# A copy from bank to bank in the first FFN layer: the second product accumulates onto the first's

## The chip, the core and the metric

The kernel runs on one core of a Trainium2 chip. The metric is the device time of one execution in microseconds (us), the median of the runs shown. Beside it stands one profiled execution with its trace: the page and the answers of the trace come from that one, and its times are counted from the start of its span.

## The reference

For x of 2048 tokens with 576 features the kernel computes `x + attention(LN(x)) @ wo + FFN(LN(x))`. The attention is local and dilated (32 heads of 18 features, 8 keys per token at a step of 2). The FFN is what the change touches:

```python
h = jnp.einsum("bsd,df->bsf", x, w1) + b1          # 576 -> 4608
sp = jnp.log1p(jnp.exp(-jnp.abs(h))) + jnp.where(h > 0, h, jnp.zeros_like(h))
act = h * jnp.tanh(sp)                               # Mish
return jnp.einsum("bsf,fd->bsd", act, w2)            # 4608 -> 576
```

## The kernel before

**Precision.** Every fp32 matrix is split into a high part and a low part, and a product is made of three matmuls per 128 rows of depth: high x high, high x low, low x high. ScalarE casts the high part (L254 for weights, L720 for activations, L807 for sums), VectorE or POOL subtracts it for the low part (L255, L721, L813).

**Halves, blocks, pairs.** The tokens are two halves (hf 0 and 1) of 1024, each of two blocks (b) of 512. The 4608 hidden features are 18 pairs (q) of two tiles (j) of 128. For one pair and one half the first layer is a 2x2 problem (block b, tile j), computed with seven products instead of eight, in the manner of Strassen and Winograd. The products are summed in three PSUM banks of 128 x 512 fp32, called cur[1], cur[2], cur[3] in the code (tag "h", four buffers) and `h` in the profile. Four more banks (tag "out") take the second layer's results `po`. A product (`prod`, L669) is six matmuls; some are followed by two more for the last 64 features (`rest`, L675).

**The parts of a pair** (`m1_part`, L727). Part 0 is the first product into bank 1, its copy to SBUF by `take` (ScalarE, L703, the tile is named c11, `c` or a raw tile in the profile), then the second product into bank 2, and `mish(hf, q, 0, 0, ...)`. Part 1 is the third product into bank 3. Part 2 accumulates onto bank 1, copied as c21; part 3 accumulates onto bank 1 again, copied as c22; part 4 accumulates onto bank 3 and part 5 onto bank 1. A pair has 50 matmuls of 512 columns.

**What `mish` does.** With a copy `t` given, VectorE adds the bank to it (L714), ScalarE applies Mish to the sum in SBUF (L715), casts it (L720), and POOL makes the low part (L721). Without one (`fresh`, block 0, tile 1), ScalarE reads the bank with Mish, and there is no add. In the second half, pairs 0 to 8, the activations are kept raw (tiles `ra`, `rm`, `rt`), and the second layer is itself a seven-product scheme: sums of raw activations (L801), high and low parts `u` (L807, L813), matmuls with prepared weights `pw` (L859, the items "N"), and adds to `accP` (L865).

**The order of the work.** A plan, a list of items, is written out in the order of TensorE's work. In the first half from pair 2 on it is: part 0, part 1, chunk, part 2, chunk, part 3, chunk, part 4, chunk, part 5, where a chunk is 24 matmuls of 288 columns of an earlier pair's second layer (L767) with its adds (L771). The last pairs of the second half have chunks too (L880, adds L883). Work of other engines hangs on the items: `bg` (loads, casts, attention steps, put there by `before`), `pend` (the rest of `mish`, run at the start of the next item, called `held` there), and `soon` (a softmax exponential with its activation table, L558, and transposes of attention, run at the start of the next item, called `first` there). Attention steps are hung on items `cuts`, worked out from the items' costs `PART` and `US`. Each engine runs its queue in the order of issue. Line 1544 ff. fixes that order within an item:

```python
for i, (fns, bg, _) in enumerate(plan):
    first, soon[:] = soon[:], []
    held, pend[:] = pend[:], []
    for fn in first + bg + (fns + held if i == at["m", 0, 1, 0] else held + fns):
        fn()
```

Of the kernel before, what the change touches and what calls it, by code (L numbers as in the profile page):

```python
# [18 lines left out]
NH = 2  # L19
# [7 lines left out]
NP = NF // 2  # L27
# [12 lines left out]
def block_kernel(ctx: ExitStack, tc: tile.TileContext, x, wq, wo, w1, b1, w2, mask, out):  # L40
    nc = tc.nc
# [624 lines left out]
    def prod(ph, wt, off, X, hi, lo, first, last):  # L666
        seq = [(off + k, wl, xs + k) for k in range(2) for wl, xs in ((0, hi), (0, lo), (1, hi))]
        for i, (wk, wl, xs) in enumerate(seq):
            nc.tensor.matmul(ph, wt[:, wl, wk * P:(wk + 1) * P], X[:, xs, :],  # L669
                             start=first and i == 0, stop=last and i == len(seq) - 1,  # L670
                             skip_group_check=True)

    def rest(ph, wt, off, X, xs):
        for wl in range(2):
            nc.tensor.matmul(ph, wt[:, wl, off * P:(off + 1) * P], X[:, xs, :], start=False, stop=wl == 1,  # L675
                             skip_group_check=True)
# [21 lines left out]
    def take(hf, q, name):  # L698
        if seven(hf, q):
            t = cur[name] = raw_act(q, *dict(c11=(0, 0), c21=(1, 0), c22=(1, 1))[name])  # L700
        else:
            t = cur[name] = sb.tile([P, TB], F32, tag="mn", bufs=5, name=f"{name}_{hf}_{q}")
        nc.scalar.copy(t, cur[1])  # L703

    def mish(hf, q, b, j, ph, t=None):
        f = 2 * (Q1[q] if hf else q) + j
        n = f"{hf}_{b}_{f}"
        fresh = t is None
        if fresh:
            t = raw_act(q, b, j) if seven(hf, q) else sb.tile([P, TB], F32, tag="mn", bufs=5, name=f"mn_{n}")  # L710

        def run():
            if not fresh:
                nc.vector.tensor_tensor(out=t, in0=ph, in1=t, op=ALU.add)  # L714
            nc.scalar.activation(t, ph if fresh else t, AF.Mish, bias=b1c[:, f:f + 1])  # L715
# [4 lines left out]
            nc.scalar.copy(a[:, 0, :], t)  # L720
            nc.gpsimd.tensor_tensor(out=a[:, 1, :], in0=t, in1=a[:, 0, :].bitcast(F32), op=ALU.subtract)  # L721
        if q or b != j:
            pend.append(run)
        else:
            late.append(run)

    def m1_part(hf, q, part):  # L727
        X0, X1 = XTs[hf, 0], XTs[hf, 1]
        if part == 5 and late:
            for fn in late[::-1]:  # L730
                fn()
            late.clear()
        wa, wc, t0, t1 = (done.get((k, hf, q)) for k in ("wa", "wc", "t0", "t1"))
        if part == 0:
            prod(bank(hf, q, 1), wa, 0, X0, 0, 5, True, True)
            take(hf, q, "c11")
            prod(bank(hf, q, 2), wa, 2, X0, 2, 7, True, False)
            rest(cur[2], wa, 4, X0, 4)
            mish(hf, q, 0, 0, cur[2], cur["c11"])
        elif part == 1:  # L740
            prod(bank(hf, q, 3), t1, 0, X1, 0, 5, True, True)
        elif part == 2:
            prod(cur[1], t0, 2, Ss[hf, 1], 0, 2, False, True)
            take(hf, q, "c21")
        elif part == 3:
            prod(cur[1], t0, 0, Ss[hf, 0], 0, 2, False, False)
            rest(cur[1], wc, 2, X1, 4)
            take(hf, q, "c22")
        elif part == 4:
            prod(cur[3], t1, 2, X1, 2, 7, False, False)  # L750
            rest(cur[3], wa, 4, X1, 4)
            mish(hf, q, 1, 0, cur[3], cur["c21"])
        else:
# [400 lines left out]
    def qi(hf, g, b, jj, alias=None):  # L1154
        add(("q", hf, g, b, jj), lambda: qkv_item(hf, g, b, jj), alias=alias)
# [4 lines left out]
    def mi(hf, q, part, alias=None):  # L1160
        add(("m", hf, q, part), lambda: m1_part(hf, q, part), alias=alias)
# [68 lines left out]
    def quad(hf, q):  # L1230
        if q == 0:
            for part, ids in ((0, (0,)), (2, (1, 2)), (1, (3, 4)), (3, (5, 6)), (5, (7, 8)), (4, (9,))):
                for p_ in {}.get(part, ()) if hf else ():
                    zi(JB - 1, p_)
                if part == 5 and hf == 0:
                    qi(hf, NQ - 1, 0, JB - 1)
                mi(hf, 0, part)
                for i in ids:
                    at["s", hf, 0, i] = len(plan) - 1
            return  # L1240
        if hf and q <= 2 * OC + 1:
            C9 = list(((1,0),(1,1),(0,0),(0,1)))
            if q == 1:
                seq = ((0, (0,)), (2, (1, 2)), (1, (3, 4)), (3, (5, 6)), (4, (7, 8)), (5, (9,)))
            elif q == 2 * OC:
                seq = ((0, (0,)), (1, (1,)), ("N", (2,)), (2, (3,)), ("N", (4,)), (3, (5,)), ("N", (6,)), (4, (7,)), ("N", (8,)),
                                (5, (9,)), ("N", ()))
            elif q == 2 * OC + 1:
                seq = (("N", (0,)), (0, ()), ("N", (1,)), (1, ()), (2, (2,)), ("C", (3,)), (3, (4,)), ("C", (5,)), (4, (6,)), ("C", (7,)), (5, (8,)), ("C", (9,)))
            elif q % 2 == 0:  # L1250
                seq = (0, 1, "N", 2, "N", 3, "N", 4, "N", 5) if q > 2 else (0, 2, "N", 1, "N", 3, "N", 4, "N", 5)
                seq = [(p_, (i,)) for i, p_ in enumerate(seq)]
            else:
                seq = [(p_, (i, 9)[0:1 + (i == 8)]) for i, p_ in enumerate((0, 1, 2, "N", 3, "N", 4, "N", 5))]
            for part, ids in seq:
                if part == "N":
                    pi()
                elif part == "C":
                    pr_(1, q - 1, *C9.pop(0))
                else:  # L1260
                    for p_ in {4:(3,)}.get(part, ()) if q == 1 else ():
                        zi(JB - 1, p_)
                    mi(1, q, part)
                for i in ids:
                    at["s", 1, q, i] = len(plan) - 1
            return
        k = 0
        late_chunks = q == 1 or (hf, q) == (1, NP - 1)
        for i, part in enumerate((0, 1, 2, None, 3, None, 4, None, 5, None) if late_chunks else
                                 (0, 1, None, 2, None, 3, None, 4, None, 5)):  # L1270
            if (hf, q) == (0, NP - 1) and i in (5, 7, 9):
                tr(0, (i - 5) // 2)
            alias = ("s", hf, q, i)
            if part is not None:
                mi(hf, q, part, alias)
            else:
                pr_(hf, q - 1, *CHUNKS[k], alias)
                k += 1
# [87 lines left out]
    for q in range(1, 2 * OC + 1):  # L1366
        i = spot(0, q, (3,2)[q > 1])
# [5 lines left out]
    i = spot(0, NP - 1, 0)  # L1373
# [5 lines left out]
    i = at["q", 1, 0, 1, 1]  # L1379
# [4 lines left out]
    i = spot(0, 9, 4)  # L1384
# [44 lines left out]
    i = at["q", 0, 1, 1, 0]  # L1429
# [3 lines left out]
    i = at["q", 0, 3, 1, 0]  # L1433
# [5 lines left out]
    i = at["q", 1, 0, 1, 1]  # L1439
# [9 lines left out]
    for n in range(0, JB, 2):  # L1449
        i = at["q", 0, 1, 0, n]  # L1450
# [4 lines left out]
    for n in range(TJ):  # L1455
        i = spot(0, 2 + n, 2)
# [3 lines left out]
    i = spot(0, NP - 2, 0)  # L1460
# [7 lines left out]
    for n, (name, pr) in enumerate((name, pr) for name in ("P4", "P5", "P2", "P3") for pr in range(2)):  # L1468
        i = items[dict(P4=0, P5=2, P3=2, P2=3)[name]][2] + pr
# [23 lines left out]
    cuts = [[], []]  # L1493
# [101 lines left out]
```

## Time and profile before

| | |
|---|---|
| three runs | 1117.51, 1117.38, 1114.83 us; median 1117.38 |
| the profiled execution | 1114.25 us |
| its span | 1112.5 us |
| granted TensorE clock, mean | 1.000 |
| matmuls of 512 columns in the first layer | 36 pairs of 50 |
| adds of VectorE at L714 on a copy `c` in SBUF | 81, 684 ns each |
| copies of a bank by ScalarE at L703 into `c` | 81, 586 ns each |

The page's first part has the engines' busy times, the fourth the chain of work that ended last. The view by stretches gives busy times of every engine between two times. The view of waits lists what an engine waited for, with total, count and the longest. The timeline lists instructions in order of start: start, duration of the row, engine, line, operation, and in brackets the idle time before it with what ended it. A row with x6 stands for six instructions in a row, and its duration reaches from the first one's start to the last one's end. PE is TensorE's matmul, PEld its weight load, DVE is VectorE, ACT is ScalarE, POOL is GpSimd. "Half 2, pair 6" is hf 1, q 6.

### The profile page before, as it was taken

To read this page: it belongs to the slowest core of one execution; us is meant where nothing else is said; L and a number is where in the kernel's file an instruction comes from. 1 tells how busy PE (TensorE), PEld (TensorE's weight loads), DVE (VectorE), ACT (ScalarE), POOL (GpSimd) and SP (SyncE) were. 2 spreads that over 40 slices of the span, in tenths; PEclk is the share of its full clock that TensorE was granted. 3 is DMA by queue.
4 is the path that set the end of the run, shared out by engine and by line. 5 is a ranking of instruction groups with operands and counts; after the bars stand their busy time and mean duration, and the time that the engine had idled before them with its cause. 6 is when DMAs were issued, how large, how long until landed. Compare 5 with 4: busy or idle time off the path is not lost.

```text
span 1112.5 us, 18203 instructions
## 1 busy us (share of the span) xinstructions
PE 1101.6 (99%) x6550; PEld 1015.2 (91%) x6550; DVE 849.5 (76%) x1367; ACT 499.5 (45%) x917; POOL 790.8 (71%) x639
## 2 busy tenths in 40 slices
PE   9999999999999999999999999999999999999998
PEld 8999899999999999999999889989989999999998
DVE  6369788888889888897656577786776677777786
ACT  5544655544454544555333354433433344343353
POOL 2479777766679688785788676666688976867532
PEclk9999999999999999999999999999999999999999
DMA  6899696868777758675597898565664657776574
GB/s 202 283 312 316 225 356 214 285 233 276 258 242 264 268 208 301 249 249 204 190 323 241 245 375 307 211 196 196 220 222 170 209 195 223 244 288 219 171 232 142
DMA packets 178270, 271.60 MB, mean 244 GB/s; under 512 B 53218, under 2 KB 120068, under 8 KB 178180
## 3 DMA queue, kind: packets, MB, share of 16 engines
q1 hardware_dynamic: 178180, 270.44, 71.6%
q8 instruction: 52, 0.85, 0.3%
q14 instruction: 38, 0.31, 0.1%
HBM read 160.39 MB, written 110.00 MB: 243 GB/s over the span
## 4 chain that ended last, share of the span: by engine, by line
PE 87%; POOL 6%; DVE 3%; issue 2%; ACT 1%; DMA 0%; SPq 0%; POOLq 0%; DVEq 0%; ACTq 0%
PE h L669 28%; PE po L767 21%; PE pq L348 9%; PE po L880 9%; PE po L859 6%; PE h L675 5%; PE o L1063 5%; PE z L446 3%; POOL pv L571 2%; POOL accP L868 1%; POOL pr L533 1%; POOL act L721 1%; POOL s L620 1%; DMA acc<-in_x 0%; PE ta L75 0%
## 5 line engine op out<-in xcount | busy, mean ns | idle before, releaser
L767 PEld LDWEIGHTS po<-w,act 128*128 128x128 f32 x1728 | 236.4, 188 | 6.0 <-POOL act L721 0.4
L767 PE MATMUL po<-w,act 128*128 128x288 f32 x1728 | 240.7, 295 | 0.1
L533 POOL TENSOR_TENSOR pr<-q,kv 128x576 f32<-128x576 f32 x128 | 196.9, 1563 | 8.5 <-DMA q<-q_d 5.0
L721 POOL TENSOR_TENSOR act<-c,act 128x512 fp32r<-128x512 f32 x81 | 107.3, 1325 | 128.6 <-ACT act L720 128.6
L571 POOL TENSOR_TENSOR pv<-L,kv 128x576 f32<-128x576 f32 x128 | 177.9, 1484 | 26.1 <-DVE L L564 21.2
L771 DVE TENSOR_TENSOR acc<-po,acc 128x288 f32<-128x288 f32 x288 | 119.4, 448 | 29.9 <-PE po L767 29.0
L348 PE MATMUL pq<-wq,xt 128*128 128x432 f32 x672 | 136.5, 361 | 1.0 <-ACT xt L81 1.0
L880 PEld LDWEIGHTS po<-w,act 128*128 128x128 f32 x960 | 130.9, 188 | 4.6 <-DVE accP L883 1.8
L880 PE MATMUL po<-w,act 128*128 128x288 f32 x960 | 133.5, 295 | 1.0 <-DVE accP L883 1.0
L348 PEld LDWEIGHTS pq<-wq,xt 128*128 128x128 f32 x672 | 125.0, 188 | 8.0 <-ACT xt L81 1.8
L715 ACT ACTIVATE c<-c,b1c 128x512 f32<-128x512 f32 x81 | 58.7, 725 | 140.7 <-DVE c L714 140.4
L669 PE MATMUL h<-xt,t 128*128 128x512 f32 x432 | 110.6, 391 | 0.5 <-DVE rt L714 0.3
L669 PE MATMUL h<-S,t 128*128 128x512 f32 x432 | 110.5, 391 | 0.0
L577 DVE TENSOR_REDUCE og<-pv 128x144 f32<-128x1152 f32 x64 | 86.0, 1345 | 25.7 <-POOL pv L571 25.6
L669 PE MATMUL h<-xt,wa 128*128 128x512 f32 x432 | 104.1, 390 | 0.0
L538 DVE TENSOR_REDUCE L<-pr 128x64 f32<-128x1152 f32 x64 | 85.8, 1341 | 23.8 <-POOL pr L533 23.7
L703 ACT COPY c<-h 128x512 f32<-128x512 f32 x81 | 47.4, 586 | 124.1 <-PE h L675 73.0
L859 PEld LDWEIGHTS po<-pw,u 128*128 128x128 f32 x672 | 92.2, 188 | 5.4 <-DVE u L813 2.1
L859 PE MATMUL po<-pw,u 128*128 128x288 f32 x672 | 94.3, 295 | 2.5 <-DVE u L813 1.6
L669 PEld LDWEIGHTS h<-xt,wa 128*128 128x128 f32 x432 | 80.9, 188 | 17.0
L669 PEld LDWEIGHTS h<-xt,t 128*128 128x128 f32 x432 | 79.0, 188 | 15.7 <-DVE rt L714 0.7
L883 DVE TENSOR_TENSOR accP<-po,accP 128x288 f32<-128x288 f32 x160 | 68.9, 452 | 29.8 <-PE po L880 28.2
(228 smaller groups left out, 1853.8 us busy)
## 6 DMA issues: line engine op xcount, KB each, us to landing
kv<-kv_d SPq DMA_DIRECT2D x64, 396.0 KB, 5.1
kept_t<-t SPq DMA_DIRECT2D x36, 512.0 KB, 4.8
t<-kept_t SPq DMA_DIRECT2D x36, 512.0 KB, 6.7
rw<-in_w SPq DMA_DIRECT2D x36, 320.0 KB, 4.4
kept_wa<-wa SPq DMA_DIRECT2D x18, 640.0 KB, 4.7
kept_w<-w SPq DMA_DIRECT2D x20, 576.0 KB, 4.1
wa<-kept_wa SPq DMA_DIRECT2D x18, 640.0 KB, 5.2
w<-kept_w SPq DMA_DIRECT2D x20, 576.0 KB, 4.1
```

Of the source, the lines that this page charges most:

```text
L348: nc.tensor.matmul(pq[:, 0:432], XT[:, xi, tok], wt[wi][:, hl, 0:432], start=i == 0, stop=i == len(seq) - 1)
L533: nc.gpsimd.tensor_tensor(out=pr[:, x:x + hh], in0=q[:, j0 + x:j0 + x + hh, None, :].to_broadcast([P, hh, W, CU]), in1=win(kt, 0, CU, j0 + ...
L538: nc.vector.tensor_reduce(L[:, k, j0:j0 + hj].rearrange("p j w h -> p (j w h)"), pr.rearrange("p j w (h d) -> p (j w h) d", h=2), axis=AX, ...
L571: nc.gpsimd.tensor_tensor(out=pr[:, x:x + hj].rearrange("p j d w -> p j w d"), in0=L[:, k, x:x + hj, :, h:h + 1].to_broadcast([P, hj, W, DH]),
L577: nc.vector.tensor_reduce(og[:, c0:c0 + DH, :].rearrange("p d j -> p j d"), pr, axis=AX, op=ALU.add)
L669: nc.tensor.matmul(ph, wt[:, wl, wk * P:(wk + 1) * P], X[:, xs, :], start=first and i == 0, stop=last and i == len(seq) - 1, skip_group_ch ...
L721: nc.gpsimd.tensor_tensor(out=a[:, 1, :], in0=t, in1=a[:, 0, :].bitcast(F32), op=ALU.subtract)
L767: nc.tensor.matmul(po, acts[hf, q, b, j][:, al, tok], done["w2", hf, 2 * q + j][:, wl, c * HC:(c + 1) * HC], start=i == 0, stop=i == 5)
L771: nc.vector.tensor_tensor(out=t, in0=po, in1=t, op=ALU.add)
L859: nc.tensor.matmul(po, units[e, k, qq][:, al, tok], w[:, qq, wl, :], start=i == 0, stop=i == 5)
L880: nc.tensor.matmul(po, acts[hf, q, b, j][:, al, tok], done["w2", hf, 2 * q + j][:, wl, c * HC:(c + 1) * HC], start=i == 0, stop=i == 5)
L883: nc.vector.tensor_tensor(out=t, in0=po, in1=t, op=ALU.add)
```

## The change

From pair 2 on, in both halves, `take` of c11 goes. ScalarE copies bank 1, which holds the first product, straight into bank 2, and the second product accumulates onto it there. `mish` for block 0, tile 0 is then fresh: ScalarE reads bank 2 with Mish, and the add goes. So that the second product needn't follow the first at once, the third product now stands between them: part 1 holds the third and then the second product. Banks are taken in the order 2, 3, 1 at the start of part 0.

```diff
-            prod(bank(hf, q, 1), wa, 0, X0, 0, 5, True, True)
-            take(hf, q, "c11")
-            prod(bank(hf, q, 2), wa, 2, X0, 2, 7, True, False)
-            rest(cur[2], wa, 4, X0, 4)
-            mish(hf, q, 0, 0, cur[2], cur["c11"])
+            for n in (2, 3, 1):
+                bank(hf, q, n)
+            prod(cur[1], wa, 0, X0, 0, 5, True, True)
+            if q > 1:
+                nc.scalar.copy(cur[2], cur[1])
+            else:
+                take(hf, q, "c11")
         elif part == 1:
-            prod(bank(hf, q, 3), t1, 0, X1, 0, 5, True, True)
+            half = (hf, q) == (1, 0)
+            prod(cur[3], t1, 0, X1, 0, 5, True, True, range(3) if half else range(6))
+        elif part == 6:
+            prod(cur[3], t1, 0, X1, 0, 5, True, True, range(3, 6))
...
+        if part == 7 or (part == 1 and q and (hf, q) != (1, 1)):
+            prod(cur[2], wa, 2, X0, 2, 7, q < 2, False)
+            rest(cur[2], wa, 4, X0, 4)
+            mish(hf, q, 0, 0, cur[2], None if q > 1 else cur["c11"])
...
-    PART = (3.2, 1.4, 1.4, 1.8, 1.8, 1.8)
+    PART = (1.4, 3.2, 1.4, 1.8, 1.8, 1.8, 0.7, 1.8)
...
+    seeded = {at["m", hf, q, 0] for hf in range(NH) for q in range(2, NP)}
     for i, (fns, bg, _) in enumerate(plan):
         first, soon[:] = soon[:], []
         held, pend[:] = pend[:], []
-        for fn in first + bg + (fns + held if i == at["m", 0, 1, 0] else held + fns):
+        if i in seeded and i not in cuts[0] + cuts[1]:
+            order = bg + held + fns + first
+        else:
+            order = first + bg + (fns + held if i == at["m", 0, 1, 0] else held + fns)
+        for fn in order:
             fn()
```

Pair 0 of both halves keeps its copy to SBUF and its add, with the second product as part 7 right behind part 0; half 2, pair 1 has it behind part 2. In half 2, pair 0, the third product is cut in two, and its second three matmuls (part 6) come between parts 3 and 5. A few items of half 2, pairs 1, 2 and 9, change places, and some attention steps move by an item. All lines behind L675 get numbers higher by 1 to 20; the copy into the bank is L740.

**TensorE and ScalarE, half 1, pair 4.** TensorE's queue at the end of pair 3 and through the first products of pair 4, before. 2226 is bank 1 of pair 4, 2235 bank 2, 2254 bank 3:

```order
L669 MATMUL h_0_3_1940<-S_0_796,wc_3_1747 128x512 x6
L675 MATMUL h_0_3_1940<-xt_1_511,wc_3_1747 128x512 x2
L669 MATMUL h_0_4_2226<-xt_0_227,wa_4_1961 128x512 x6
L669 MATMUL h_0_4_2235<-xt_0_227,wa_4_1961 128x512 x6
L675 MATMUL h_0_4_2235<-xt_0_227,wa_4_1961 128x512 x2
L669 MATMUL h_0_4_2254<-xt_1_511,t_0_4_2132 128x512 x6
```

The same place in the change (2225 is bank 1, 2223 bank 2, 2224 bank 3):

```order
L670 MATMUL h_0_3_1941<-S_0_796,wc_3_1746 128x512 x6
L676 MATMUL h_0_3_1941<-xt_1_511,wc_3_1746 128x512 x2
L670 MATMUL h_0_4_2225<-xt_0_227,wa_4_1952 128x512 x6
L670 MATMUL h_0_4_2224<-xt_1_511,t_0_4_2130 128x512 x6
L670 MATMUL h_0_4_2223<-xt_0_227,wa_4_1952 128x512 x6
L676 MATMUL h_0_4_2223<-xt_0_227,wa_4_1952 128x512 x2
```

The third product's six matmuls moved ahead of the second product's eight. ScalarE's queue around the copy of the first product, before (`L_1` is a softmax tile, `w`, `wa` and `t` are weights of later pairs, `mn_0_7` is tile 1 of pair 3, `c_0_4` is c11 of pair 4):

```order
L558 ACT_TABLE_LOAD
L558 ACTIVATE L_1_1599<-L_1_1599 128x256
L254 CAST w_0_8_2214<-rw_8_2071 128x576
L715 ACT_TABLE_LOAD
L715 ACTIVATE mn_0_7_2212<-h_0_3_1940,b1c 128x512
L720 CAST act_0_7_2223<-mn_0_7_2212 128x512
L703 COPY c_0_4_2233<-h_0_4_2226 128x512
L254 CAST wa_5_2247<-rw_10_2136 128x640
L715 ACTIVATE c_0_4_2233<-c_0_4_2233,b1c 128x512
```

And in the change:

```order
L254 CAST w_0_8_2211<-rw_8_2069 128x576
L716 ACTIVATE mn_0_7_2210<-h_0_3_1941,b1c 128x512
L721 CAST act_0_7_2220<-mn_0_7_2210 128x512
L740 COPY h_0_4_2223<-h_0_4_2225 128x512
L558 ACT_TABLE_LOAD
L558 ACTIVATE L_1_1599<-L_1_1599 128x256
L254 CAST wa_5_2237<-rw_10_2134 128x640
L254 CAST w_0_9_2254<-rw_9_2132 128x576
L716 ACT_TABLE_LOAD
L716 ACTIVATE mn_0_8_2253<-h_0_4_2223,b1c 128x512
```

The exponential and its table moved behind the copy, which now ends in a bank, and the Mish of tile 0 reads that bank.

**TensorE, half 2, pair 0** (the change of halves). Before, from the third product on (7248 is bank 1, 7290 bank 3):

```order
L669 MATMUL h_1_0_7290<-xt_1_6439,t_1_1_7072 128x512 x6
L669 MATMUL h_1_0_7248<-S_1_6575,t_1_1_7049 128x512 x6
L675 MATMUL h_1_0_7248<-xt_1_6439,wc_1_7089 128x512 x2
L669 MATMUL h_1_0_7248<-S_1_6663,wc_1_7089 128x512 x6
L675 MATMUL h_1_0_7248<-xt_1_6439,wc_1_7089 128x512 x2
```

In the change (7226 is bank 1, 7225 bank 3):

```order
L670 MATMUL h_1_0_7225<-xt_1_6427,t_1_1_7048 128x512 x3
L670 MATMUL h_1_0_7226<-S_1_6559,t_1_1_7025 128x512 x6
L676 MATMUL h_1_0_7226<-xt_1_6427,wc_1_7073 128x512 x2
L670 MATMUL h_1_0_7225<-xt_1_6427,t_1_1_7048 128x512 x3
L670 MATMUL h_1_0_7226<-S_1_6647,wc_1_7073 128x512 x6
L676 MATMUL h_1_0_7226<-xt_1_6427,wc_1_7073 128x512 x2
```

Three of the third product's matmuls now stand between two groups that go onto bank 1.

**VectorE, half 2, pair 6.** Before, around the low part `u_0_1` that the second layer's next product reads (`ra_7255` is c11 of pair 6, `og`, `oT` are attention):

```order
L801 TENSOR_TENSOR rm_7261<-rt_7264,rm_7261 128x512
L577 TENSOR_REDUCE og_1_8154<-pv_1_1_1_8380 128x8x18
L714 TENSOR_TENSOR ra_7255<-h_1_6_8441,ra_7255 128x512
L593 STREAM_TRANSPOSE oT_1_8471<-og_1_8154 128x576
L813 TENSOR_TENSOR u_0_1_8452<-rm_7262,u_0_1_8452 128x512
```

In the change:

```order
L811 TENSOR_TENSOR rm_7239<-rt_7242,rm_7239 128x512
L577 TENSOR_REDUCE og_1_8135<-pv_1_1_1_8360 128x8x18
L593 STREAM_TRANSPOSE oT_1_8449<-og_1_8135 128x576
L823 TENSOR_TENSOR u_0_1_8425<-rm_7240,u_0_1_8425 128x512
L811 TENSOR_TENSOR rm_7240<-rt_7243,rm_7240 128x512
```

The add of the second product is gone from between the reduction and the low part.

More of the change, by code (lines that the diff above doesn't have):

```diff
@@ L664, in bank, with prod @@
         return cur[n]
-    def prod(ph, wt, off, X, hi, lo, first, last):
+    def prod(ph, wt, off, X, hi, lo, first, last, some=range(6)):
         seq = [(off + k, wl, xs + k) for k in range(2) for wl, xs in ((0, hi), (0, lo), (1, hi))]
-        for i, (wk, wl, xs) in enumerate(seq):
+        for i in some:
+            wk, wl, xs = seq[i]
             nc.tensor.matmul(ph, wt[:, wl, wk * P:(wk + 1) * P], X[:, xs, :],
@@ L752, in m1_part @@
             mish(hf, q, 1, 0, cur[3], cur["c21"])
-        else:
+        elif part == 5:
             prod(cur[1], wc, 0, Ss[hf, 2], 0, 2, False, False)
@@ L1236, in quad @@
                     qi(hf, NQ - 1, 0, JB - 1)
+                elif part == 5:
+                    mi(hf, 0, 6)
                 mi(hf, 0, part)
+                if part == 0:
+                    mi(hf, 0, 7)
                 for i in ids:
@@ L1243, in quad @@
             if q == 1:
-                seq = ((0, (0,)), (2, (1, 2)), (1, (3, 4)), (3, (5, 6)), (4, (7, 8)), (5, (9,)))
+                seq = ((0, (0,)), (1, (1,)), (2, (2,)), (7, (3, 4)), (3, (5, 6)), (4, (7, 8)), (5, (9,)))
             elif q == 2 * OC:
@@ L1248, in quad @@
             elif q == 2 * OC + 1:
-                seq = (("N", (0,)), (0, ()), ("N", (1,)), (1, ()), (2, (2,)), ("C", (3,)), (3, (4,)), ("C", (5,)), (4, (6,)), ("C", (7,)), (5, (8,)), ("C", (9,)))
+                seq = (("N", (0,)), (0, ()), (1, ()), ("N", (1,)), (2, (2,)), ("C", (3,)), (3, (4,)), ("C", (5,)), (4, (6,)), ("C", (7,)), (5, (8,)), ("C", (9,)))
             elif q % 2 == 0:
-                seq = (0, 1, "N", 2, "N", 3, "N", 4, "N", 5) if q > 2 else (0, 2, "N", 1, "N", 3, "N", 4, "N", 5)
+                seq = (0, 1, "N", 2, "N", 3, "N", 4, "N", 5)
                 seq = [(p_, (i,)) for i, p_ in enumerate(seq)]
```

## Prediction

> **What bounds the kernel now.** I read the page first: shares of the engines, then the chain that ended last.
>
> ```profile
> PE 1101.6 (99%) x6550; PEld 1015.2 (91%) x6550; DVE 849.5 (76%) x1367; ACT 499.5 (45%) x917; POOL 790.8 (71%) x639
> PE 87%; POOL 6%; DVE 3%; issue 2%; ACT 1%; DMA 0%; SPq 0%; POOLq 0%; DVEq 0%; ACTq 0%
> ```
>
> TensorE is busy for 1101.6 of 1112.5 us, and 87% of the last chain is its matmuls. So it does nothing for 10.9 us in all, and the rest goes only if matmuls go. Busy time by stretches says where the 10.9 us lie.
>
> ```profile
> 200.00:400.00 200.00, 200.00 (x1213) 183.28 (x1212) 175.44 (x279) 98.01 (x158) 146.92 (x121) 1.00 0.77 263
> 560.00:700.00 140.00, 137.62 (x717) 125.05 (x716) 91.52 (x119) 56.95 (x125) 105.77 (x78) 1.00 0.88 293
> ```
>
> The columns are the stretch, its length, then busy time and instructions of PE, PEld, DVE, ACT and POOL, and the granted clock (1.00). Where VectorE is fullest (175.44 of 200 us) TensorE has no idle time at all; 2.4 us of it lie around the change of halves. Next, what TensorE waited for.
>
> ```profile
> PE po L859 <- DVE u L813: 1.6, 1, 1.6
> PE po L880 <- DVE accP L883: 1.0, 1, 1.0
> PE po L859 <- ACT u L807: 0.8, 1, 0.8
> PE h L669 <- ACT rt L703: 0.7, 1, 0.7
> PE h L669 <- DVE rt L714: 0.3, 1, 0.3
> PE h L669 <- DVE c L714: 0.2, 1, 0.2
> ```
>
> These six waits hold 4.6 us and are the ones within the FFN. A change that moves VectorE and ScalarE work can win some of these 4.6 us, and can lose without such a limit. The view counts only what is left of a wait behind the weight load, so below I take each loss from start to start.
>
> [...]
>
> **The change, part by part.** These groups price the operations:
>
> ```profile
> L714 DVE TENSOR_TENSOR c<-h,c 128x512 f32<-128x512 f32 x81 | 55.3, 684 | 25.2 <-PE h L675 12.3 <-ACT c L703 12.1
> L703 ACT COPY c<-h 128x512 f32<-128x512 f32 x81 | 47.4, 586 | 124.1 <-PE h L675 73.0 <-PE h L669 50.4
> L925 ACT COPY ot<-o 128x512 f32<-128x512 f32 x8 | 4.7, 581 | 0.0
> L715 ACT ACTIVATE c<-c,b1c 128x512 f32<-128x512 f32 x81 | 58.7, 725 | 140.7 <-DVE c L714 140.4
> L715 ACT ACTIVATE mn<-h,b1c 128x512 f32<-128x512 f32 x27 | 18.6, 687 | 23.9 <-PE h L675 23.9
> ```
>
> *Removed:* 32 adds of the second product (pairs 2 to 17 of two halves) at 684 ns, 21.9 us of VectorE, which falls from 849.5 to about 828. TensorE feels that only where an add stood ahead of something it waited for. *Replaced:* 32 Mish that read SBUF (725 ns) by 32 that read the bank (687), 1.2 us of ScalarE less, off the path. *Replaced:* 32 copies from a bank to SBUF by copies from a bank to a bank, which no row has. The nearest rows bound it: 581 (L925, from SBUF into a bank) and 586 (L703). I take 0.58 us, so the copy costs nothing by itself; a copy slower by the whole 0.58 would be the case of the slower rival. TensorE's matmuls are as many and as wide as before: 0.
>
> *Added: one wait per pair.* The second product can't start before the copy ends, and everything else of TensorE's queue stands behind it, so a microsecond of lateness is a microsecond of the kernel. The cover is the third product, six matmuls. The usual case, in the first half and in the second's last pair:
>
> ```profile
> 211.48 2.88 PE L669 MATMUL h<-xt,wa 128*128 128x512 f32 x12
> 214.20 0.61 PE L675 MATMUL h<-xt,wa 128*128 128x512 f32 x2
> ...
> 211.68 0.69 ACT L715 ACTIVATE mn<-h,b1c 128x512 f32<-128x512 f32 x1 [1.08 <-PE h L675]
> 212.40 0.62 ACT L720 CAST act<-mn 128x512 fp32r<-128x512 f32 x1
> 213.03 0.59 ACT L703 COPY c<-h 128x512 f32<-128x512 f32 x1
> ```
>
> ```profile
> 1017.28 2.89 PE L669 MATMUL h<-xt,wa 128*128 128x512 f32 x12
> ...
> 1018.90 0.59 ACT L703 COPY c<-h 128x512 f32<-128x512 f32 x1
> ```
>
> The first two products start at 211.48 and the next group at 214.20: 12 matmuls in 2.72 us, 0.227 each. The first product is done at about 213.0; ScalarE has worked off the Mish and the cast of the pair before just then, and copies from 213.03 to 213.62. With the third product between, the second would start at 211.48 + 12 x 0.227 = 214.20: **0.58 us to spare**. In the last pair it is 1020.00 against 1019.49, so 0.51. Of the 32 copies, worked out in this way from the first quoted to the last, 25 have 0.5 to 0.6 us and three 0.2 to 0.35. Four are late, by 3.6, 2.4, 0.5 and 0.1. The worst:
>
> ```profile
> 187.40 2.88 PE L669 MATMUL h<-xt,wa 128*128 128x512 f32 x12
> 190.12 0.61 PE L675 MATMUL h<-xt,wa 128*128 128x512 f32 x2
> ...
> 190.61 1.28 ACT L715 ACT_TABLE_LOAD   x1
> 191.90 0.69 ACT L715 ACTIVATE mn<-h,b1c 128x512 f32<-128x512 f32 x1
> 193.15 0.58 ACT L703 COPY c<-h 128x512 f32<-128x512 f32 x1
> ```
>
> Here a softmax exponential and two table loads stood ahead of the copy. Its end, 193.73, is 3.6 us behind 190.12 (and the matmuls still have their 0.227 us, 2.72 for 12). The order of the changed kernel puts the copy ahead of the exponential, in this pair and in pair 12 of the second half (2.4 us), so these two cost 0: what stands ahead is Mish and cast, as in the usual case. The exponentials start some 0.6 us later instead; their attention work is POOL's, with 71% busy. The third late one remains:
>
> ```profile
> 452.64 2.88 PE L669 MATMUL h<-xt,wa 128*128 128x512 f32 x12
> ...
> 452.48 1.24 ACT L254 CAST w<-rw 128x576 fp32r<-128x576 f32 x2
> 453.63 0.55 ACT L398 CAST zhT<-zB 128x432 fp32r<-128x432 f32 x1
> 455.32 0.58 ACT L703 COPY c<-h 128x512 f32<-128x512 f32 x1
> ```
>
> Three casts stand ahead of Mish, cast and copy, and all of them still do. The copy ends at 455.90, the need is 452.64 + 2.72 = 455.36: 0.54 late. VectorE, whose adds ScalarE followed there, is up to one add (0.68) further on, so between 0 and 0.54; I take 0.3. The fourth, 0.1 late, I count in full. **Loss 0.4 us.**
>
> *Waits that shrink.* (a) The second-layer product of pair 6, second half, waits for a low part that stands behind one of the removed adds:
>
> ```profile
> 747.83 1.35 PEld L859 LDWEIGHTS po<-pw,u 128*128 128x128 f32 x10 [0.33 <-DVE u L813]
> 745.82 0.69 DVE L714 TENSOR_TENSOR ra<-h,ra 128x512 f32<-128x512 f32 x1
> 747.12 0.65 DVE L813 TENSOR_TENSOR u<-rm,u 128x512 fp32r<-128x512 f32 x1
> ```
>
> Without 0.69 of VectorE ahead all 0.33 goes. (b) At the change of halves, pair 0's next product waits for the copy of the bank it adds to:
>
> ```profile
> 632.19 0.63 PE L675 MATMUL h<-xt,wc 128*128 128x512 f32 x2
> 633.49 1.66 PE L669 MATMUL h<-S,wc 128*128 128x512 f32 x6 [0.68 <-ACT rt L703]
> ```
>
> It was due at 632.19 + 2 x 0.227 = 632.64 and starts at 633.49. The change puts three matmuls of the third product into that hole: -0.68. (c) and (d) Twice a product waits for an add that isn't removed but stands in a queue that gets shorter:
>
> ```profile
> 781.51 1.63 PE L669 MATMUL h<-xt,t 128*128 128x512 f32 x6 [0.29 <-DVE rt L714]
> 865.54 1.63 PE L669 MATMUL h<-xt,t 128*128 128x512 f32 x6 [0.24 <-DVE c L714]
> 863.53 1.35 DVE L577 TENSOR_REDUCE og<-pv 128x144 f32<-128x1152 f32 x1 [1.32 <-POOL pv L571]
> 864.80 0.68 DVE L714 TENSOR_TENSOR c<-h,c 128x512 f32<-128x512 f32 x1
> ```
>
> Six matmuls in a row would have 2.88 - 6 x 0.227 = 1.52 us; these have 1.63, so each stop costs 0.1 us more at the restart, and with the weight load's part of the wait about 0.55 in all. In the first, low parts ahead of the add wait for ScalarE's casts, which no longer stand behind a Mish that waits for an add; in the second a reduction waits for POOL, which starts earlier if its exponential does, and that one no longer stands behind such a Mish either. Between 0 and 0.55 each; I take 0.55 for both. **Gain 0.33 + 0.68 + 1.1 = 2.1 us.** The two longest waits I leave as they are: u L813 (1.6) hangs on a chain of ScalarE and VectorE steps that gets back about what it loses by being moved, accP L883 (1.0) on sums behind POOL.
>
> **The sum:** -2.1 + 0.4 = -1.7 us. The profiled execution took 1114.25 us (span 1112.5 and 1.75 around it) and would take 1112.6. The median of the three runs shown is 3.1 us higher, 1117.38; on that basis **1115.7 us**.
>
> **The rivals.** *All waits go:* the freer queues bring every wait of the FFN to nothing and no copy is late: -4.6, **1112.8**. For it: four of the six name VectorE. Against: the two longest stand behind POOL or behind ScalarE's casts, which stay. *Nothing changes:* the added 0.4 and a missed (c) and (d) leave -0.6, **1116.8**. For it: VectorE waits for others anyway, 140 us of Mish waits notwithstanding. *The copies are late (slower):* place, ScalarE's queue ahead of the copy. Mish and cast of the pair before take 1.35 us, the first product 1.36, so the copy starts on time with nothing to spare, and one further cast (0.67) ahead of it in a pair takes all of the 0.52 to 0.58. A pair like that of 455 us costs 0.54 + 0.1 for the restart. From about eight such pairs on (8 x 0.64 = 5.1 against -1.7) the kernel is slower by more than 0.3%; with 10 it would be +4.7, **1122.1**; a bank-to-bank copy twice as long would make all 32 late by about 0.05 and, with the restarts, do the same. Against it: the order keeps ahead of each copy what stood there. *It doesn't do what it says:* if the second product overwrote the copied bank, each engine would still run the same instructions in the same time, so this has no time of its own.
>
> **How the numbers follow.** 0.3% is 3.35 us, about what a measurement of this kernel can tell from no change. The forecast (1114.2 to 1117.0: both ends of the lateness, of (c) and of (d)) has 0.52; nothing changes, 0.16; all waits go, 0.19; late copies, 0.13. So faster by over 0.3% (under 1114.0) has 0.19 + 0.02 of the forecast's edge = 0.21, slower (over 1120.7) 0.13, within 0.66. The range reaches down past 1112.8, since some restarts go too, to 1112.0, and up to 1119.8, half of the late copies: about 0.2 stays outside.
>
> **What would show it.** Right: VectorE's row falls to about 828 us with 32 fewer L714 rows, TensorE's stays at 1101 to 1102; the second product starts 2.72 us after the first in at least 28 pairs; the wait at 633 is under 0.25 and that at 747 is gone. Wrong: a line of h waiting for ScalarE's bank copy, many times, in the view of waits; a bank copy well over 0.6 us; a new wait for a bank at the start of a pair, since the banks change their order; a longer 1.0 for accP because exponentials came later.

## The result, and the profile after

The change is slower: 1122.89 us median (1121.63 to 1123.71) against 1116.9, ratio 1.0055 with a 95% interval from 1.004 to 1.0069. The prediction was 1115.7 us, with a range that ended at 1119.8. In the later runs the kernel before stood lower, at 1114.3 to 1114.6 us; against that level the change would be at about 1.0075, so its ratio can be 0.2% low beside those of the experiments. The profiled execution of the change took 1123.71 us, with a span of 1121.3 (before 1112.5). The shares on its page:

```profile
PE 1104.0 (98%) x6550; PEld 1016.2 (91%) x6550; DVE 839.1 (75%) x1335; ACT 499.3 (45%) x917; POOL 794.1 (71%) x639
```

VectorE has its 32 instructions less, but TensorE's idle time grew from 10.9 to 17.3 us, and its busy time by 2.4. Two stretches of the change:

```profile
200.00:400.00 200.00, 200.00 (x1212) 182.95 (x1211) 167.84 (x271) 97.84 (x158) 145.33 (x118) 1.00 0.76 263
700.00:900.00 200.00, 193.67 (x1162) 176.92 (x1161) 144.40 (x221) 74.59 (x118) 146.80 (x108) 0.99 0.57 197
```

And the second one in the kernel before:

```profile
700.00:900.00 200.00, 198.55 (x1197) 180.73 (x1196) 146.80 (x237) 77.80 (x121) 151.32 (x111) 1.00 0.59 203
```

From 200 to 400 us, where eight pairs copy from bank to bank, TensorE stays at 200.00. Most of the loss is between 700 and 900: 6.3 us idle where it was 1.4, and the granted clock isn't 1.00. TensorE's waits of the change:

```profile
PE po L890 <- DVE accP L893: 4.8, 2, 3.8
PE po L869 <- ACT u L817: 2.4, 1, 2.4
...
PE h L670 <- DVE rt L715: 1.1, 1, 1.1
PE h L670 <- DVE c L715: 0.6, 1, 0.6
PE h L670 <- ACT h L740: 0.4, 1, 0.4
...
PE h L670 <- DMA t<-kept_t: 0.2, 1, 0.2
```

The wait that the change adds, for the bank copy (L740), is among the smallest of these. The largest is for an add to accP, which the change doesn't touch. The timelines of TensorE, POOL and VectorE around it, at pair 9 of half 2:

```profile
837.77 0.62 PE L676 MATMUL h<-xt,wc 128*128 128x512 f32 x2
842.25 4.98 PE L890 MATMUL po<-w,act 128*128 128x288 f32 x24 [3.85 <-DVE accP L893]
```

```profile
833.65 2.82 POOL L878 TENSOR_TENSOR accP<-accP,accP 128x576 f32<-128x576 f32 x2
836.43 1.28 POOL L832 TENSOR_TENSOR act<-rm,act 128x512 fp32r<-128x512 f32 x1
837.68 2.77 POOL L533 TENSOR_TENSOR pr<-q,kv 128x576 f32<-128x576 f32 x2
```

```profile
840.48 1.35 DVE L538 TENSOR_REDUCE L<-pr 128x64 f32<-128x1152 f32 x1 [8.32 <-POOL pr L533]
841.75 1.54 DVE L893 TENSOR_TENSOR accP<-po,accP 128x288 f32<-128x288 f32 x4
```

Read from below: the four adds to accP, which free the "out" banks, stand in VectorE's queue behind a reduction of attention (L538). That one stands idle for 8.32 us until POOL has made its two products `pr`, and POOL makes them behind two sums of accP and a low part, 4.0 us of work. TensorE's next chunk was due at 837.77 + 2 x 0.227 = 838.22 and starts at 842.25, 4.03 us late. The same place in the kernel before, TensorE and then POOL:

```profile
833.78 0.63 PE L675 MATMUL h<-xt,wc 128*128 128x512 f32 x2
834.28 3.45 PE L880 MATMUL po<-w,act 128*128 128x288 f32 x24
```

```profile
829.66 2.81 POOL L533 TENSOR_TENSOR pr<-q,kv 128x576 f32<-128x576 f32 x2
833.70 2.80 POOL L868 TENSOR_TENSOR accP<-accP,accP 128x576 f32<-128x576 f32 x2
```

There the two products stand ahead of the two sums, and the chunk starts 0.05 us behind its due time of 834.23. In the change the chunk is not only late but then runs slowly:

```profile
842.00:846.00 4.00, 3.75 (x18) 3.75 (x19) 2.70 (x7) 0.72 (x1) 4.00 (x4) 0.61 0.02 5
```

The granted clock is 0.61 in the four us after the wait. The chunk's 24 matmuls take 4.98 us; chunks of the same trace that no wait precedes, the one at 876.22 for instance, take 3.33, a step of 0.132 us and 0.295 for the last. So the slow clock costs another 1.65 us, and the place 5.7 in all. Of the 8.8 us between the two profiled spans another 1.6 is the wait for ACT u, to which the last section comes back.

### The profile page after: what moved, and what is told of

It reads as the page before. It is cut to its first block, busy times and chain, and to the rows that moved or that the text cites. A ratio compares the mean times of both kernels' runs of the same rounds, so it can differ in the third digit from the quotient of the medians.

```text
span 1121.3 us, 18105 instructions
## 1 busy us (share of the span) xinstructions
PE 1104.0 (98%) x6550; PEld 1016.2 (91%) x6550; DVE 839.1 (75%) x1335; ACT 499.3 (45%) x917; POOL 794.1 (71%) x639
## 4 chain that ended last, share of the span: by engine, by line
PE 89%; DVE 4%; POOL 3%; ACT 2%; issue 1%; DMA 0%; SPq 0%; DVEq 0%; ACTq 0%; POOLq 0%
PE h L670 28%; PE po L777 20%; PE po L890 11%; PE pq L348 9%; PE po L869 8%; PE h L676 5%; PE o L1073 5%; PE z L446 3%; POOL pv L571 1%; POOL s L620 1%; DVE u L823 1%; POOL pr L533 1%; DMA acc<-in_x 0%; PE ta L75 0%; DVE L L538 0%
## 5 line engine op out<-in xcount | busy, mean ns | idle before, releaser
L722 POOL TENSOR_TENSOR act<-c,act 128x512 fp32r<-128x512 f32 x56 | 73.7, 1316 | 128.0 <-ACT act L721 124.4
L781 DVE TENSOR_TENSOR acc<-po,acc 128x288 f32<-128x288 f32 x288 | 122.1, 451 | 44.4 <-PE po L777 43.6
L670 PE MATMUL h<-xt,wa 128*128 128x512 f32 x432 | 109.9, 390 | 0.4 <-ACT h L740 0.4
L538 DVE TENSOR_REDUCE L<-pr 128x64 f32<-128x1152 f32 x64 | 85.8, 1342 | 26.5 <-POOL pr L533 26.4
L704 ACT COPY c<-h 128x512 f32<-128x512 f32 x56 | 32.9, 587 | 132.1 <-PE h L676 77.5
L670 PEld LDWEIGHTS h<-S,t 128*128 128x128 f32 x432 | 77.7, 188 | 13.3 <-ACT rm L704 0.5
```

The costliest lines, as they stand in the source:

```text
L538: nc.vector.tensor_reduce(L[:, k, j0:j0 + hj].rearrange("p j w h -> p (j w h)"), pr.rearrange("p j w (h d) -> p (j w h) d", h=2), axis=AX, ...
L781: nc.vector.tensor_tensor(out=t, in0=po, in1=t, op=ALU.add)
```

## The experiments

The theory (A in the expectations): the loss is this one place, and it comes from an attention step that moved in POOL's queue, not from the copy. The rivals: every pair loses a little at its copy (B); or POOL is late there anyway (C). In each run the kernel before was run beside it, at 1114.3 to 1114.6 us; ratios are to that.

**Only the attention step put back.** In the change's list of items of pair 9, spot 1, on which an attention step hangs, had followed its "N" behind part 1. It goes to part 1 itself:

```diff
-seq = (("N", (0,)), (0, ()), (1, ()), ("N", (1,)), (2, (2,)), ...
+seq = (("N", (0,)), (0, ()), (1, (1,)), ("N", ()), (2, (2,)), ...
```

> The change as it is, but the attention step of pair 9 of half 2 hangs on the item of part 1 instead of the second-layer product behind it. TensorE's order stays that of the change; on POOL two products of attention move ahead of two sums of accP and a low part. Theory A (the loss is one stall at 838 us: POOL's two attention products come late, VectorE's reduction waits for them, the adds of accP wait behind it, TensorE waits 4.0 us and then runs about 16 matmuls at half clock): the stall and the half clock go, 5.8 us, from 1122.9 to about 1117. Theory B (the loss is the new wait of each pair for the copy): nothing changes, 1122.9. Theory C (POOL is late here anyway, since it began its sums 1 us later): the stall shrinks to about 2 us and the half clock goes, about 1119.

Measured: 1115.61 us, ratio 1.0011 (1.0003 to 1.002). Its TensorE, POOL and VectorE at the same place:

```profile
835.52 0.61 PE L676 MATMUL h<-xt,wc 128*128 128x512 f32 x2
836.04 3.46 PE L890 MATMUL po<-w,act 128*128 128x288 f32 x24
```

```profile
831.43 2.80 POOL L533 TENSOR_TENSOR pr<-q,kv 128x576 f32<-128x576 f32 x2
834.20 2.82 POOL L878 TENSOR_TENSOR accP<-accP,accP 128x576 f32<-128x576 f32 x2
```

```profile
834.26 1.35 DVE L538 TENSOR_REDUCE L<-pr 128x64 f32<-128x1152 f32 x1 [4.33 <-POOL pr L533]
835.53 1.54 DVE L893 TENSOR_TENSOR accP<-po,accP 128x288 f32<-128x288 f32 x4
```

Two instructions of POOL change places with three others, and the wait is down to 0.07 us (due at 835.97), with no slow clock behind it (the chunk takes 3.46 us). Of the 0.55% that the change lost, 0.11 are left. Theory B, by which nothing would have changed, is out as the cause. The ratio by itself wouldn't decide between A (about 1117 on a kernel before at 1116.9, ratio 1.0001) and C (1119, 1.0019): it lies between them. The trace does: C left a wait of about 2 us at this place.

**Pair 9 wholly as before.** The items stand as before, `("N", (0,)), (0, ()), ("N", (1,)), (1, ()), ...`.

> The change with the items of pair 9 of half 2 in the order of before (product of the second layer between parts 0 and 1), so that TensorE's order, too, goes back there. Theory A: as with the attention step alone, about 1117, within 1 us of that run. Theory B: 1122.9. If TensorE's order at pair 9 and not POOL's is what counts, this one is at 1117 and the other stays near 1123.

Measured: 1115.77 us, 1.0009 (1.0 to 1.0018), the same as with the step alone. Within the noise of these two runs TensorE's order at pair 9 doesn't matter; the step's does.

**The kernel before with the change's pair 9 and nothing else.** The edit goes the other way round:

```diff
-seq = (("N", (0,)), (0, ()), ("N", (1,)), (1, ()), (2, (2,)), ...
+seq = (("N", (0,)), (0, ()), (1, ()), ("N", (1,)), (2, (2,)), ...
```

> The kernel before with nothing but the change's item order at pair 9 of half 2 (its adds, its copies to SBUF stay). Theory A: it alone makes the kernel before slower, by 3 to 6 us, with a wait for accP near 832 us; 1120 to 1123. Theory B: no copy into a bank, so no loss, 1116.9.

Measured: 1122.08 us, 1.0061 (1.0046 to 1.0076). This kernel has no copy into a bank at all and is about as slow as the change: 7.5 us above the kernel before, where 3 to 6 were expected. Its trace has the same wait, longer yet:

```profile
836.62 0.63 PE L675 MATMUL h<-xt,wc 128*128 128x512 f32 x2
842.35 1.09 PE L880 MATMUL po<-w,act 128*128 128x288 f32 x3 [5.10 <-DVE accP L883]
```

The chunk is 5.28 us late (due at 837.07), and the granted clock is 0.57 from 842 to 846. The profiled execution also has a wait of 1.3 us for accP at 689 us that neither the kernel before nor the change has; what brought it wasn't settled.

**The exponential ahead of the copy.** The new order within an item is taken out of the change (`if False:` in place of the test for `seeded`).

> The change with the old order within an item, so that the exponential and its table stand ahead of the copy. By the prediction's rows two copies become late by 3.6 and 2.4 us: about +6 on the change, 1129, with waits for ScalarE's bank copy at pair 4 of half 1 and pair 12 of half 2. Theory A says so too, since the stall at 838 stays. If the exponentials' place were behind the loss of the change (attention later, so POOL later), it would be faster than the change, about 1119.

Measured: 1130.92 us, 1.0145 (1.0131 to 1.0159). That is 8.0 us above the change's median, or 10 by the two ratios, whose kernels before stood at different levels; about 6 were expected. Its waits and its pair 4 of half 1:

```profile
PE h L670 <- ACT h L740: 6.1, 3, 3.4
PE po L890 <- DVE accP L893: 4.8, 2, 3.9
```

```profile
189.91 1.52 PE L670 MATMUL h<-xt,t 128*128 128x512 f32 x6
194.85 1.93 PE L670 MATMUL h<-xt,wa 128*128 128x512 f32 x6 [3.41 <-ACT h L740]
```

```profile
195.00:198.50 3.50, 3.50 (x13) 2.95 (x14) 1.84 (x2) 1.82 (x4) 2.01 (x2) 0.66 0.40 151
```

Due at 189.91 + 1.36 = 191.27, the second product is 3.58 us late; the prediction had 3.6 for this copy from the trace of before. The other one, in pair 12 of half 2, is 2.41 late (due at 912.78, start at 915.19), where it had 2.4. What it had not is the slow clock behind these waits, 0.66 in the row above. The stall at 838 stays (3.9 in the view), and the kernel isn't faster, so the later exponentials weren't behind the change's loss. So reading the lateness of a copy from the trace of the kernel before was sound, and so was the finding that the new order removes it.

**No cover.** With the attention step put back, the second product stands right behind the copy, and the third behind it:

```diff
             if q > 1:
                 nc.scalar.copy(cur[2], cur[1])
+                prod(cur[2], wa, 2, X0, 2, 7, False, False)
+                rest(cur[2], wa, 4, X0, 4)
+                mish(hf, q, 0, 0, cur[2])
...
-        if part == 7 or (part == 1 and q and (hf, q) != (1, 1)):
+        if part == 7 or (part == 1 and q == 1 and (hf, q) != (1, 1)):
```

> The change with the attention step of pair 9 put back (the run before, 1.0011 of the kernel before) and the second product right behind the copy, the third product behind it: the cover of six matmuls taken away. Theory A (the copy is free only under its cover): in each of 32 pairs TensorE waits from the first product's last start to the copy's end, about 0.04 + 0.58 + 0.16 + 0.1 for the restart = 0.9 us, more in the few with casts ahead: 28 to 32 us in all, ratio 1.024 to 1.028. Theory B (TensorE has slack of its own that takes such waits): under 5 us, ratio below 1.005.

Measured: 1146.13 us in two executions, 1.0283 (1.0264 to 1.0302). Its waits for the bank copy, and pair 5 of half 1, TensorE and then ScalarE:

```profile
PE h L670 <- ACT h L740: 23.9, 32, 1.8
```

```profile
214.69 1.52 PE L670 MATMUL h<-xt,wa 128*128 128x512 f32 x6
216.87 1.66 PE L670 MATMUL h<-xt,wa 128*128 128x512 f32 x6 [0.66 <-ACT h L740]
```

```profile
216.25 0.57 ACT L740 COPY h<-h 128x512 f32<-128x512 f32 x1
```

The wait comes 32 times. The second product was due at 214.69 + 1.36 = 216.05 and starts at 216.87, 0.82 late, and 0.1 goes at the restart: about 0.9 per pair as expected. Against the run with only the step put back (1.0011) the six matmuls of the third product, placed between, take away about 30 us.

**The first pairs back.** What is left, 0.11%, should lie in pairs 0 and 1, where the change moved products without a bank copy: the waits of 1.1 (rt) and 0.6 (c) in the change's list. They go back to the code of before:

```diff
             else:
                 take(hf, q, "c11")
+                prod(cur[2], wa, 2, X0, 2, 7, True, False)
+                rest(cur[2], wa, 4, X0, 4)
+                mish(hf, q, 0, 0, cur[2], cur["c11"])
...
-        if part == 7 or (part == 1 and q and (hf, q) != (1, 1)):
+        if part == 1 and q > 1:
```

The items, the banks' order and the costs of the parts of these pairs go back with them. One thing of the change stays, though the expectation says "in every way": in half 2, pair 0, the third product is still cut in two.

> The change with the attention step of pair 9 put back, and pairs 0 and 1 of both halves in every way as before (second product right behind the first, banks in order 1, 2, 3, costs of parts as before); pairs 2 on keep the bank copy. If the rest of the loss comes from the moves in pairs 0 and 1 (waits of 0.8 us at 128 us and 1.24 us at 648 us), these go to the 0.3 and 0.2 us of before: 1.5 us less than with the step alone, ratio 0.9985 to 1.0000. If it comes from pairs 2 on, the ratio stays at 1.001.

Measured: 1114.35 us, 0.9999 (0.9989 to 1.0009), inside the expected range, but not only by what was expected. Both waits are gone, and in the profiled execution another has come, with a slow clock behind it (0.62 from 655 to 659), where pair 2 of half 2 needs its weights t:

```profile
651.22 1.52 PE L670 MATMUL h<-xt,wa 128*128 128x512 f32 x6
654.95 2.02 PE L670 MATMUL h<-xt,t 128*128 128x512 f32 x6 [2.20 <-DVE og L577]
```

Due at 652.58, the third product is 2.37 us late. The profile names an instruction of VectorE, a reduction of attention; it writes nothing that this product reads. What the product does need is t, and the trace of the change has its load as the releaser of a wait (0.2 us) at this place. In this run that load is issued at 645.64, 6.9 us ahead of its need; in the kernel before it was issued at 644.75 and used at 659.88, behind part 2 and a whole product of the second layer. The DMA engines are full there (1.07 from 651 to 655). The load of t issued before it, at 642.72, landed 9.4 us later; as long a time from 645.64 gives 655.0, and the product starts at 654.95. That it is the load is argued from this, and wasn't tried by itself. The slow clock isn't in every execution of this kernel: four of eleven have a mean clock of 0.998 and take 1115.91 to 1117.14 us, the profiled one among them; the median one has 1.000.

**Casts behind the copy.** On top of it, loads and casts of an item stand behind the copy, and pair 2 of half 2 has its old order of items (part 2 ahead of the third product):

```diff
-            order = bg + held + fns + first
+            order = held + fns + bg + first
...
-                seq = (0, 1, "N", 2, "N", 3, "N", 4, "N", 5)
+                seq = (0, 1, "N", 2, "N", 3, "N", 4, "N", 5) if q > 2 else (0, 2, "N", 1, "N", 3, "N", 4, "N", 5)
```

> The run with the first pairs back, and besides: casts and loads of an item stand behind the bank copy instead of ahead of it (pairs 2 on, items without an attention step), and pair 2 of half 2 has its old order of items. By the trace the late copies of pairs 9 and 15 of half 1 (0.16 and 0.60, 0.2 for their restarts) and most of the wait for t at 654 us (0.4) go: about 1.3 us less, ratio 0.9975 to 0.999. If the casts' later place hurts VectorE's low parts, new waits for w or t appear and the gain is gone.

Measured: 1115.91 us, 1.0013 (1.0004 to 1.0021): a miss. The late copy of pair 15 of half 1 is cured, the one of pair 9 isn't (0.16 late as before), and pair 2 of half 2 has no cover in that order:

```profile
650.28 1.52 PE L670 MATMUL h<-xt,wa 128*128 128x512 f32 x6
652.72 1.66 PE L670 MATMUL h<-S,t 128*128 128x512 f32 x6 [0.92 <-ACT h L740]
654.21 0.82 PE L872 MATMUL po<-pw,u 128*128 128x288 f32 x5
657.22 3.75 PE L872 MATMUL po<-pw,u 128*128 128x288 f32 x19 [2.18 <-DVE u L826]
```

Part 2 accumulates onto bank 1 and so waits until the copy has read it (due at 651.64, 1.08 late). The wait for u behind it grew to 2.2 in the view, 2.35 from start to start, and the clock fell again (0.70 from 657.2 to 661).

**From pair 3 on in half 2.** So pair 2 of half 2 goes back to the copy to SBUF and the add, too; 31 pairs keep the bank copy:

```diff
-            if q > 1:
+            if q > 1 + hf:
                 nc.scalar.copy(cur[2], cur[1])
...
-        if part == 1 and q > 1:
+        if part == 1 and q > 1 + hf:
```

> As the run with the first pairs back, but pair 2 of half 2 is as before, too (copy to SBUF, add, old order of its products and items), so 31 pairs keep the bank copy; casts and loads of an item stand behind the copy. If the bank copy pays where the work around it stays in place, what is left of the kernel before's waits is: 0.3 at 120, 0.3 and 0.35 at the change of halves, about 1.8 at 655, 1.0 at 817, 1.2 at 1049 us, and those at 747, 781 and 865 are gone; no half clock. That is 1.2 to 1.5 us less than before, ratio 0.9985 to 0.9990. If a freer VectorE brings nothing, or the late copies come back in other pairs, the ratio is 1.000 or above.

Measured: 1113.23 us against 1114.58, 0.9988 (0.9978 to 0.9998), the fastest kernel of the study. Of TensorE's waits in the FFN three are left:

```profile
PE po L872 <- DVE u L826: 1.6, 1, 1.6
...
PE po L893 <- DVE accP L896: 1.0, 1, 1.0
PE po L872 <- ACT u L820: 0.9, 1, 0.9
```

They are the three longest of the kernel before, at about their old size; the shorter three are gone from the view. From start to start the profiled execution gains 0.33 us at the change of halves, 0.40 at 747, 0.47 at 781 and 0.39 at 865, 1.6 of the 1.8 us by which its span is shorter. The last three, 1.26 us, come at the three places where the wait named VectorE. The 0.33 isn't the bank copy's: it comes with the third product cut in two in pair 0, which this kernel keeps. The gain is 0.12% with an interval that ends at 0.02%, so it is small and just clear of noise; the cut of the third product alone wasn't tried.

## Why the prediction was wrong

**The step that failed** is in the sum. The prediction went through the new wait, the shorter queues and the waits that shrink, and said of the wait for accP: "The two longest waits I leave as they are". It took the moved items of half 2 for free. One of them, the "N" of pair 9, carried an attention step with it, and the step's two products went behind 4.0 us of other work in POOL's queue. At this place the kernel before has no wait for accP at all; the 1.0 us that the prediction left alone is a later one, near 1047. The terms are 4.03 us of wait and 1.65 of slow clock, with 0 in the prediction for both. The two runs with one edit each show it from both sides: taking the step back from the change leaves 1.0011 of 1.0055, and giving pair 9 to the kernel before makes 1.0061. Going through every instruction that a moved item issues, and every queue it is moved past, would have led to POOL's queue. Among its signs of being wrong the prediction had a longer wait for accP, but as the old 1.0 grown longer, and because of later exponentials; that one is unchanged (0.99), and the exponentials weren't the cause.

**The slow clock** was in no case of the prediction. It counted a restart of 0.1 us behind a wait and nothing more.

**The new wait** was found in the right places, at about half its size. The view has 0.4 us in one place, and the prediction's 0.4 agrees with that by luck only, since it counts from start to start. That place is the copy that it had at 0 to 0.54 late, and took at 0.3:

```profile
455.37 1.52 PE L670 MATMUL h<-xt,t 128*128 128x512 f32 x6
457.33 1.65 PE L670 MATMUL h<-xt,wa 128*128 128x512 f32 x6 [0.44 <-ACT h L740]
```

Due at 455.37 + 1.36 = 456.73, the second product is 0.60 late, a little more than the upper end: a VectorE with one add less didn't bring ScalarE forward there. Pair 9 of half 1 is 0.16 late, and each of the two pays 0.1 at the restart, so about 1.0 us in all. In half 2, pair 2, the second product follows a wait for t and is 0.42 late; in the other 29 pairs it starts 2.72 us after the first, so the sign of at least 28 pairs was met. The price of the copy itself was right, too, a little below both bounds:

```profile
L740 ACT COPY h<-h 128x512 f32<-128x512 f32 x32 | 18.3, 572 | 6.6 <-PE h L670 6.3
```

**The waits that shrink** came at 747, 781 and 865 us of the kernel before: in the change no such wait is left there, and from start to start they give 0.28, 0.47 and 0.39 us (forecast 0.33, 0.55 and 0.55). The fourth, at 633, fell as well, but the change of halves gains 0.33 us and not 0.68: the two groups that follow the halves of the third product start 0.20 and 0.16 us late. So the gain is about 1.5 us and not 2.1, and these terms can't explain the miss. The lower end of the forecast, 1114.2, doesn't follow from the ends that it names; they reach from 1115.4 to 1117.0.

**VectorE's busy time** fell by 10.4 us and not by 21.9, although 32 adds are gone. The trace says where the rest is. The durations of all its rows, summed, fall by 17.1 us (914.1 to 897.0), so other instructions took 4.8 us longer, low parts `u` above all; one of these is the row of 4.47 us in the last section, on which a wait of TensorE hangs. Another 6.7 us are a matter of counting: rows in a run overlap, and busy time counts an overlap once.

**What was not priced at all:** the products that moved in pairs 0 and 1, where nothing is copied from bank to bank. The 1.1 us for rt (at 648) and the 0.6 for c (at 129) are theirs; with these pairs back both are gone.

**The slower rival** had the right side and the wrong mechanism: it priced late copies at 0.64 each and needed eight, and the change has two. That its 1122.1 us lies next to the measured 1122.89 is luck. The run without cover shows that late copies would have cost about what it said (0.9 per pair there, where the whole copy is bare).

## What to carry to other kernels

A list of work items that says when one engine does what also says when everything hung on the items is issued, on every engine. Where a change moves an item, compare all the queues and not only those of the engines that the change is about; here two rows of POOL's queue made 0.44 of the 0.55% that the change lost. A new wait, on the other hand, can be priced from the trace of the kernel before to some tenths of a us, by when its condition would have been fulfilled and what then stands between. And a wait can cost TensorE more than its length: behind the one of 4.03 us the chunk took 1.65 us longer, with a granted clock of 0.61; behind one of 2.62 us in the same trace the clock stayed at 1.00.

## What the runs showed of the hardware

**A wait of 2.35 us had a slow clock behind it, and one of 2.62 us had none.** Waits are counted from start to start here, beyond the matmuls' step. After waits of 5.28 us (the kernel before with pair 9), 4.03 (the change), 4.06, 3.58 and 2.41 (exponential first), 2.37 (first pairs back) and 2.35 (casts behind the copy) the clock fell. After one of 2.62 us in the change it didn't: the second group below was due at 814.75 + 24 x 0.132 = 817.92, starts at 820.54, and takes 3.41 us.

```profile
814.75 3.38 PE L869 MATMUL po<-pw,u 128*128 128x288 f32 x24
820.54 3.41 PE L869 MATMUL po<-pw,u 128*128 128x288 f32 x24 [2.41 <-ACT u L817]
```

Between the start and the end of the traces a slow stretch is 3.41 us long, at a granted clock of 0.50 (the change's from 842.90 to 846.32); one, with the exponential first, is twice as long. In that trace slow stretches start at 196.09, 844.62 and 916.30, which are 190 and 21 times 3.413 us apart. The one of the change starts 245 times 3.413 us behind 6.64, where its clock first rises to 1.00. So each trace is divided here into such stretches, counted from that first rise; that the clock goes by them is an estimate from these starts. Two of them with what followed, first from the run with casts behind the copy, then from the change:

```profile
655.27:658.68 3.41, 1.46 (x11) 1.46 (x12) 3.38 (x3) 0.88 (x3) 3.41 (x3) 1.00 1.03 378
658.68:662.09 3.41, 3.41 (x14) 3.12 (x14) 1.44 (x2) 1.65 (x5) 2.54 (x3) 0.50 1.05 388
```

```profile
819.01:822.42 3.41, 1.88 (x14) 1.91 (x15) 3.41 (x7) 0.53 (x1) 0.00 (x0) 1.00 0.85 292
822.42:825.83 3.41, 3.41 (x21) 3.06 (x20) 2.80 (x6) 1.09 (x2) 2.75 (x2) 1.00 0.24 81
```

With TensorE busy for 1.46 of 3.41 us (57% idle) the next stretch is slow; with 1.88 (45% idle) it isn't: the 2.62 us lie across 819.01, 1.09 of them before it and 1.53 behind. Two more places agree: in the change the stretch from 839.49, with 0.65 us busy (81% idle), is followed by the slow one from 842.90; in the kernel before the one from 655.77, with 1.91 us busy (44% idle), is followed by one at 1.00. All other full-speed stretches of these two traces are idle for 37% or less, and none has a slow one behind it. What happens between 45% and 57%, no run shows, nor why the stretch from 844.62 with the exponential first, slow itself and 43% idle, is followed by a second slow one. It also fits that with the first pairs back the clock fell in some executions only, four of eleven; that wasn't tried by itself.

**The same instruction at 4.47 and 1.66 us.** The wait for ACT u L817, 2.4 us in the change's profile, is 0.8 in the run with only the step put back, with the same queues up to there. Behind it stands one low part of VectorE; the change's row, then that run's:

```profile
813.74 4.47 DVE L823 TENSOR_TENSOR u<-ra_r,u 128x512 fp32r<-128x512 f32 x1 [0.20 <-ACT u L817]
```

```profile
813.07 1.66 DVE L823 TENSOR_TENSOR u<-ra_r,u 128x512 fp32r<-128x512 f32 x1 [0.20 <-ACT u L817]
```

POOL works without a pause beside both. In the change it makes a sum and two products, from 813.56 to 817.65 us. VectorE's row begins at 813.74, ahead of the two products at 814.80, and ends behind them, at 818.21. In the other run VectorE's row ends at 814.73, and POOL's two products, from 814.12, take 3.73 us where they take 2.85 in the change. So one trace has the long row on VectorE and the other has it on POOL; what decides which, no run shows. TensorE's wait differs by 1.6 us between the two. In the kernel before the same row takes 1.64 us and in the run from pair 3 on 1.67, with 3.73 us for POOL's two products in both.
